# Moving the loads of a large key-value cache from SyncE's hardware queue to GpSimd's software queue in a two-block attention decode kernel

## The chip, the cores and the metric

The kernel runs on one core of one Trainium2 chip. The metric is the time of one execution in device microseconds (us). The profile's span is about 2 us shorter than the time (1326.8 us of span for 1329.2 us).

## The reference

One token attends to two caches, and the two outputs are concatenated. Block A is plain attention with 32 heads over 32,768 keys each. (Below, P·V is the product of a head's softmax weights with its values.) Block B has 32 query heads over 8 key heads and looks at the last 4,096 keys only.

```python
def _A_ref(x, k_cache, v_cache, wq, wo):          # x [1,1,512], caches [1,32,32768,128] bf16
    q = (x @ wq) ...                              # 32 heads of 128
    p = softmax(q · k_cache * Dh ** -0.5)
    return (p · v_cache) ... @ wo
# _B_ref: the same with 8 key heads, W = min(4096, max(256, Sk // 4)) last keys
return jnp.concatenate([a, b], axis=-1)
```

A's keys and values are 2 x 32 loads of 8.39 MB, 537 MB in all. Everything else (both wq, B's keys and values, both wo) is 33.6 MB.

## The kernel before

The program is a list of operations per engine; a wait is put in wherever an operation names another as its dependency. Each load names the operations that last read its buffer. `kbuf` has three thirds of 4.19 MB; a head of A takes two neighbouring ones, so every head shares one third with the next. `vbuf` holds one head's values, or B's values in two halves.

```python
    def load(self, dst, src, sem, *deps):
        self.op("sp", lambda e: e.dma_start(dst, src).then_inc(sem, 16), *deps)
    ...
    def k_thirds(self, g):
        return (1, 0) if g % 2 == 0 else (1, 2)

    def load_k(self, g, parts):                   # parts == 2 only for the last head
        ...
        if parts == 1:
            self.load(self.kbuf[:, w * lo:w * lo + 2 * w], src, self.mark("k", 0), *free)
            ...
        else:
            for i, t in enumerate(self.k_thirds(g)):
                self.load(self.kbuf[:, w * t:w * t + w], src[:, w * (t - lo):w * (t - lo) + w], self.mark("k", i), *free)

    def load_v(self, g):
        self.load(self.vbuf[:, :], self.kv_src("v", "A", g)[:, 0, :], self.mark("v", 0), *self.free["v"])
    ...
        for g in range(2):
            ...
            self.load_b("v", g)                   # block B's values
            self.emit_PV("B", g)
        ...
        for g in range(NQH):                      # block A, head by head
            self.load_k(g, 1 if g < NQH - 1 else 2)
            self.load_v(g)
            ...
            self.emit_unit("A", g)                # transposes of keys, scores
            self.emit_stats("A", g)
            self.emit_PT("A", g)
            self.emit_PV("A", g)
        for n in ("B", "A"):                      # output weights
            for part in range(len(self.WO_CUTS[n]) - 1):
                self.load_wo(n, part)
```

All loads but two of 1 KB are on one queue, SyncE's. So the order of this list is the order in which the loads are served, whatever each load waits for.

## Time and profile before

| | before |
|---|---|
| time, median | 1329.17 us (1329.11 to 1329.23) |
| bytes read, mean rate | 570.4 MB, 430 GB/s |
| busy: transfer engines, TensorE, VectorE | 99.6%, 73%, 57% |
| one head of A in the middle | 38.70 us (two loads of 19.35) |
| start of the first head of A, of the second-last, of the last | 83.45, 1246.03, 1279.71 us |

The numbers to read in such a profile are these: the share of the queue that carries the loads (the bound), the starts of heads (where time is lost or won), and the time from a load's issue to its landing (how far ahead it was asked for). The lines are in the prediction.

### The profile page before, as it was taken

The page shows a single profiled execution, that of the slowest core. Times are in us where ns is not written, and L with a number is a line of the kernel's source. Part 1 is how long each engine was busy: PE and PEld are TensorE (multiplying, and loading weights), DVE is VectorE, ACT ScalarE, POOL GpSimd, SP SyncE. Part 2 cuts the span into 40 slices and gives each one's busy share as a digit, 9 for nine tenths or more (in the row PEclk, how much of TensorE's full clock was granted, in tenths as well). Part 3 has the DMA queues.
Part 4 walks back from the last instruction along what each step waited for, and adds up shares of the span by engine and source line. Part 5 has one row for each costly group of instructions (what it writes and reads, how often), then busy time and mean ns, then how long its engine had stood idle before and what let it go on. Part 6 is the DMA issues. An engine that isn't in the chain of part 4 may idle for free.

```text
span 1326.8 us, 28797 instructions
## 1 busy us (share of the span) xinstructions
PE 964.5 (73%) x13436; PEld 679.5 (51%) x13436; DVE 749.8 (57%) x1345; ACT 54.8 (4%) x167; POOL 2.3 (0%) x17
## 2 busy tenths in 40 slices
PE   3757678777667877766787777678777767877786
PEld 3544455554445555444565544456554445655453
DVE  3645466665456666545666645566654556665473
ACT  0000000000000000000000000000000000000000
POOL 0000000000000000000000000000000000000000
PEclk9877788887788888778888878888887888888798
DMA  9999999999999999999999999999999999999998
GB/s 394 431 431 438 432 433 433 437 429 433 433 435 437 433 435 431 433 433 435 437 433 435 431 433 433 431 441 433 431 435 433 431 433 441 433 431 435 433 431 344
DMA packets 13079, 570.66 MB, mean 430 GB/s; under 512 B 1540, under 2 KB 1544, under 8 KB 1928
## 3 DMA queue, kind: packets, MB, share of 16 engines
q1 hardware_dynamic: 12776, 570.43, 99.6%
q8 instruction: 12, 0.20, 0.1%
q10 hardware_dynamic: 288, 0.00, 0.0%
q14 instruction: 3, 0.02, 0.0%
HBM read 570.43 MB, written 0.00 MB: 430 GB/s over the span
## 4 chain that ended last, share of the span: by engine, by line
DMA 70%; PE 28%; DVE 1%; issue 0%; SPq 0%; ACT 0%
DMA kbuf<-in_A_k_cache_dram 65%; PE psT L491 23%; PE psS L513 4%; DMA kbuf<-in_B_k_cache_dram 3%; DMA kbuf<-in_A_wo_dram 3%; DVE kt L494 1%; PE psACC L593 0%; SPq L286 0%; DVE oc_A L609 0%; ACT psb L541 0%; DVE tr_in L530 0%; PE psPT L565 0%; ACT ptsb L568 0%; PE psPT L655 0%; PE psG L620 0%
## 5 line engine op out<-in xcount | busy, mean ns | idle before, releaser
L494 DVE COPY kt<-psT 128x1024 bf16<-128x1024 bf16 x1056 | 655.2, 684 | 245.0 <-PE psT L491 243.1
L491 PE MATMUL psT<-ident,kbuf 128*128 128x128 bf16 x8448 | 579.2, 234 | 176.2 <-DMA kbuf<-in_A_k_cache_dram 164.4
L491 PEld LDWEIGHTS psT<-ident,kbuf 128*128 128x128 bf16 x8448 | 539.7, 106 | 268.2 <-DMA kbuf<-in_A_k_cache_dram 172.5
L593 PE MATMUL psACC<-vbuf,ptsb 128*4 128x512 bf16 (+1 forms) x2112 | 183.2, 523 | 23.1 <-ACT ptsb L568 21.3
L513 PE MATMUL psS<-kt,qw 128*32 128x512 bf16 x2048 | 157.6, 385 | 15.5 <-DVE kt L494 15.5
L607 DVE TENSOR_SCALAR oc_A<-psACC,hot_A 128x128 f32<-128x128 f32 x32 | 11.2, 351 | 247.8 <-PE psG L620 247.8
L593 PEld LDWEIGHTS psACC<-vbuf,ptsb 128*4 128x4 bf16 (+1 forms) x2112 | 60.0, 110 | 136.9 <-issue 87.2
L541 ACT ACTIVATE psb<-psS,nb_A 128x512 bf16<-128x512 f32 x32 | 22.0, 687 | 1169.9 <-DVE nb_A L540 1169.9
L513 PEld LDWEIGHTS psS<-kt,qw 128*32 128x32 bf16 x2048 | 34.0, 95 | 58.0 <-DVE kt L494 31.4
L620 PE MATMUL psG<-oc_A,hw 128*32 128x128 f32 (+1 forms) x128 | 19.3, 227 | 52.3 <-DVE oc_A L609 52.3
L620 PEld LDWEIGHTS psG<-oc_A,hw 128*32 128x32 f32 x128 | 11.4, 109 | 62.4 <-DVE oc_A L609 55.0
L565 PE MATMUL psPT<-ident,psb 128*128 128x128 bf16 x136 | 17.9, 274 | 34.0 <-ACT psb L541 34.0
L609 DVE SCALAR_TENSOR_TENSOR oc_A<-psACC,hot_A,oc_A 128x128 f32<-128x128 f32 x96 | 33.7, 351 | 3.4
L530 DVE TENSOR_REDUCE tr_in<-psS 128x1 f32<-128x512 f32 x34 | 23.5, 692 | 17.1 <-PE psS L513 17.1
L565 PEld LDWEIGHTS psPT<-ident,psb 128*128 128x128 bf16 x136 | 10.0, 116 | 37.0 <-ACT psb L541 36.7
L534 PE MATMUL psACC<-rows,tr_in 128*1 128x64 f32 x64 | 8.7, 217 | 25.6 <-DVE tr_in L530 25.6
L568 ACT ACTIVATE ptsb<-psPT 128x512 bf16<-128x512 bf16 x34 | 20.3, 597 | 28.2 <-PE psPT L565 28.2
L534 PEld LDWEIGHTS psACC<-rows,tr_in 128*1 128x1 f32 x64 | 2.7, 81 | 35.1 <-DVE tr_in L530 35.1
L538 PE MATMUL psACC<-mr_A,nscale 1*128 1x1 f32 x64 | 12.1, 256 | 9.8 <-DVE mr_A L537 9.8
L538 PEld LDWEIGHTS psACC<-mr_A,nscale 1*128 1x128 f32 x64 | 9.4, 183 | 15.7 <-DVE mr_A L537 15.7
L540 DVE COPY nb_A<-psACC 128x1 f32<-128x1 f32 x32 | 5.1, 158 | 15.0 <-PE psACC L538 15.0
L537 DVE TENSOR_REDUCE mr_A<-psACC 1x1 f32<-1x64 f32 x32 | 6.8, 213 | 11.7 <-PE psACC L534 11.7
(71 smaller groups left out, 75.1 us busy)
## 6 DMA issues: line engine op xcount, KB each, us to landing
kbuf<-in_B_k_cache_dram SPq DMA_DIRECT2D x2, 4096.0 KB, 32.5
vbuf<-in_B_v_cache_dram SPq DMA_DIRECT2D x2, 4096.0 KB, 23.6
kbuf<-in_A_k_cache_dram SPq DMA_DIRECT2D x2, 4096.0 KB, 22.0
vbuf<-in_B_wq_dram SPq DMA_DIRECT2D x1, 4096.0 KB, 12.3
vbuf<-in_A_wq_dram SPq DMA_DIRECT2D x1, 4096.0 KB, 32.4
kbuf<-in_B_wo_dram SPq DMA_DIRECT2D x2, 2048.0 KB, 33.1
kbuf<-in_A_wo_dram SPq DMA_DIRECT2D x1, 1408.0 KB, 28.5
kbuf<-in_A_wo_dram SPq DMA_DIRECT2D x1, 1024.0 KB, 30.6
```

The costliest lines, as they stand in the source:

```text
L491: inst = e.transpose(T[:, 128 * k:128 * k + 128], src[:, DH * k:DH * k + DH], self.ident[:, :])
L494: self.copies.append(self.op("dve", lambda v: v.tensor_copy(KT[:, :], T[:, :]), o, to="pe"))
L513: inst = e.matmul(self.S[32 * c:32 * c + 32, :], lhsT=win, rhs=self.kt[(bb + c // 2) % NKT][:, 512 * (c % 2):512 * (c % 2) + 512], start=b ...
L530: o = dve(lambda v: v.reduce_max(tr["in"][:, 0:1], self.S[:, :], axis=AXX), self.sdone, self.k_pool, to="pe" if name == "A" else None)
L534: o = self.op("pe", lambda e: e.matmul(self.ACC[0:1, 0:64], lhsT=tr["in"][:, 0:1], rhs=self.rows64[:, :], start=True, stop=True, skip_grou ...
L538: o = self.op("pe", lambda e: e.matmul(self.ACC[:, 64:65], lhsT=self.nscale[:, :], rhs=t["mr"][0:1, :], start=True, stop=True, skip_group_ ...
L541: self.sread = self.op("act", lambda s: s.activation(out=self.psb[:, :], in_=self.S[:, :], func=ACTF.Exp, bias=t["nb"][:, k:k + 1], scale= ...
L565: inst = e.transpose(PT[:, 128 * jj:128 * jj + 128], self.psb[:, 128 * jj:128 * jj + 128], self.ident[:, :])
L568: self.ptread = self.op("act", lambda s: s.activation(out=self.ptsb[:, :], in_=PT[:, 0:512], func=ACTF.Copy), self.psread, to="pe")
L593: inst = e.matmul(acc[32 * c:32 * c + rows, 0:512], lhsT=lhsT, rhs=rhs, start=begin, stop=end, tile_position=(0, 32 * c), skip_group_check ...
L609: o = self.op("dve", lambda v, src=src, hot=hot: v.scalar_tensor_tensor(out=oc, in0=src, scalar=hot, in1=oc, op0=ALU.mult, op1=ALU.add), p ...
L620: return self.op("pe", lambda e: e.matmul(self.G[0:32, c0 + c:c0 + c2], lhsT=win, rhs=t["oc"][g % 2][:, c:c2], start=False, stop=True, ski ...
```

## The change

The intent is to hand the bulk loads to GpSimd, which is idle, and whose queue has its descriptors (the orders to the transfer engines) built in software; the profile lists it as `software_dynamic`. GpSimd waits for each load's semaphore and raises another (`kasem`, `vasem`) for TensorE: a relay. The core of the diff (cut):

```diff
     def load(self, dst, src, sem, *deps):
-        self.op("sp", lambda e: e.dma_start(dst, src).then_inc(sem, 16), *deps)
+        self.op(self.queue, lambda e: e.dma_start(dst, src).then_inc(sem, 16), *deps)
...
+    def swload(self, which, g, dst, deps):
+        sem = self.swsem[which]
+        src = self.kv_src(which, "A", g)[:, 0, :]
+        self.op("pool", lambda e: e.dma_start(dst, src).then_inc(sem, 16), *deps)
+
+    def swlanded(self, which, g):
+        sem = self.mark(which, 0)
+        self.op("pool", lambda e: e.sem_inc(sem, 16), (self.swsem[which], 16 * (g + 1)))
...
-        if parts == 1:
-            self.load(self.kbuf[:, w * lo:w * lo + 2 * w], src, self.mark("k", 0), *free)
...
+        self.swload("k", g, self.kbuf[:, w * lo:w * lo + 2 * w], [self.free["k"][t] for t in self.k_thirds(g)])
+        if g:
+            self.swlanded("v", g - 1)
     def load_v(self, g):
-        self.load(self.vbuf[:, :], self.kv_src("v", "A", g)[:, 0, :], self.mark("v", 0), *self.free["v"])
+        self.swload("v", g, self.vbuf[:, :], self.free["v"])
+        self.swlanded("k", g)
...
+        self.queue = "pool"
...
-            self.load_k(g, 1 if g < NQH - 1 else 2)
+            self.load_k(g)
...
         self.loop = {}
+        self.queue = "sp"
```

B's loads and the output weights stay on SyncE. The last head's keys, two loads before, are one load now.

More of the change, by code (lines that the diff above doesn't have):

```diff
@@ L276, in alloc @@
         s = nc.alloc_semaphore
+        self.kasem = [s(f"kasem{i}") for i in range(2)]
+        self.vasem = [s(f"vasem{i}") for i in range(2)]
+        self.swsem = {w: s(f"swsem_{w}") for w in "kv"}
         self.ksem = [s(f"ksem{i}") for i in range(2)]
@@ L310, in k_thirds, with load_k @@
         return (1, 0) if g % 2 == 0 else (1, 2)
-    def load_k(self, g, parts):
+    def swload(self, which, g, dst, deps):
[5 more added lines that the diff above has]
+        self.op("pool", lambda e: e.sem_inc(sem, 16), (self.swsem[which], 16 * (g + 1)))
+    def load_k(self, g):
         w = HALF * DH
-        src = self.kv_src("k", "A", g)[:, 0, :]
         lo = min(self.k_thirds(g))
-        free = [self.free["k"][t] for t in self.k_thirds(g)]
-        if parts == 1:
-            self.load(self.kbuf[:, w * lo:w * lo + 2 * w], src, self.mark("k", 0), *free)
-            sem = self.mark("k", 1)
-            self.op("sp", lambda e: e.sem_inc(sem, 16))
-        else:
-            for i, t in enumerate(self.k_thirds(g)):
-                self.load(self.kbuf[:, w * t:w * t + w], src[:, w * (t - lo):w * (t - lo) + w], self.mark("k", i), *free)
+        self.swload("k", g, self.kbuf[:, w * lo:w * lo + 2 * w], [self.free["k"][t] for t in self.k_thirds(g)])
+        if g:
+            self.swlanded("v", g - 1)
     def load_v(self, g):
-        self.load(self.vbuf[:, :], self.kv_src("v", "A", g)[:, 0, :], self.mark("v", 0), *self.free["v"])
+        self.swload("v", g, self.vbuf[:, :], self.free["v"])
+        self.swlanded("k", g)
     WQ_SLOT = {"B": 0, "A": 1}
@@ L377, in plan @@
         self.emit_spread("B")
+        self.queue = "pool"
+        self.lsem = {"k": self.kasem, "v": self.vasem}
+        self.fill = {w: [0, 0] for w in "kv"}
         for g in range(NQH):
             self.loop = {"pe": g // 2, "dve": g // 2}
-            self.load_k(g, 1 if g < NQH - 1 else 2)
+            self.load_k(g)
             self.load_v(g)
+            if g == NQH - 1:
+                self.swlanded("v", g)
             self.emit_qcopy(g)
@@ L388, in plan @@
         self.loop = {}
+        self.queue = "sp"
         for n in ("B", "A"):
@@ L474, in emit_unit @@
             for half in range(2):
-                self.emit_T(HALF * lo + 16 * st + 8 * half, self.landed("k", g if name == "B" else i), t)
+                self.emit_T(HALF * lo + 16 * st + 8 * half, self.landed("k", g) if name == "B" else (self.kasem[0], 16 * (g + 1)), t)
             if n % 2:
@@ L595, in mm @@
             return inst
-        pv = self.op("pe", mm, self.landed("v", 0 if name == "A" else g), self.ptread, self.accread, to="sp")
+        pv = self.op("pe", mm, (self.vasem[0], 16 * (g + 1)) if name == "A" else self.landed("v", g), self.ptread, self.accread,
+                     to="pool")
         for i in (0, 1) if name == "A" else (g,):
```

## The prediction

> **What bounds the kernel now.** I read the busy rows and the queue table first, then the chain of work that ended last, then the waits, and last the timeline of one middle head and of the tail.
>
> ```profile
> DMA  9999999999999999999999999999999999999998
> ...
> DMA packets 13079, 570.66 MB, mean 430 GB/s; under 512 B 1540, under 2 KB 1544, under 8 KB 1928
> ...
> q1 hardware_dynamic: 12776, 570.43, 99.6%
> ...
> DMA 70%; PE 28%; DVE 1%; issue 0%; SPq 0%; ACT 0%
> ```
>
> The reader sees 16 transfer engines busy in every slice, one queue (SyncE's, q1) accounting for 99.6% of their time. The chain names PE for 28%, but only because a load is followed back to the read that freed its buffer. The waits settle it:
>
> ```profile
> PE psT L491 <- DMA kbuf<-in_A_k_cache_dram: 164.4, 31, 12.9
> ```
>
> TensorE stands still before the keys of nearly every head, about 5.3 us each; the loads are late, not the engines. The middle of the trace (one head, 39 us):
>
> ```profile
> core 0: us, PE busy (x) PEld busy (x) DVE busy (x) ACT busy (x) POOL busy (x), PEclk, DMA share, GB/s
> ...
> 600.00:639.00 39.00, 28.55 (x416) 20.65 (x413) 23.11 (x42) 1.59 (x5) 0.00 (x0) 0.87 1.00 434
> ```
>
> TensorE is busy 28.6 of 39 us, the transfer engines all of it, at 434 GB/s. Heads repeat every 38.7 us (TensorE starts at 626.71 here and at 665.42 for the next): two loads of 8.39 MB each, so 19.35 us a load. GpSimd is idle.
>
> How far ahead are the loads queued? The time from issue to landing less the 19.35 us of transfer is the time a load waited behind the one before it, which is the slack before the engines would run dry:
>
> ```profile
> vbuf<-in_A_v_cache_dram SPq DMA_DIRECT2D x32, 26.5
> ...
> kbuf<-in_A_k_cache_dram SPq DMA_DIRECT2D x31, 27.8
> ...
> x_B<-in_B_x_dram ACTq DMA_DIRECT2D x1, 1.0 KB, 12.5
> ```
>
> Slack is 26.5 - 19.35 = 7.2 us for values, 27.8 - 19.35 = 8.5 us for keys. The timeline agrees:
>
> ```profile
> 619.20 0.33 SPq L286 DMA_DIRECT2D vbuf<-in_A_v_cache_dram  x1
> ...
> 626.71 5.53 PE L491 MATMUL psT<-ident,kbuf 128*128 128x128 bf16 x64 [5.49 <-DMA kbuf<-in_A_k_cache_dram]
> ...
> 637.49 0.33 SPq L286 DMA_DIRECT2D kbuf<-in_A_k_cache_dram  x1
> ```
>
> The values' load is issued at 619.20, 7.5 us before the keys ahead of it land (626.71); the next keys' at 637.49, 8.6 us before those values land (626.7 + 19.35 = 646.1).
>
> **What the Trainium skill says.** (1) "DMA: Bandwidth & Descriptors", Issuing engines are not separate DMA queues: loads from any issuer run on the same 16 engines; another issuer saves only issue time. Consistent with this trace, where issuing costs 0.33 us every 19 us and q1 alone fills the engines. (2) Same page, Latency and other measured facts: first byte about 0.6 us for the hardware path, 1 us for the software path. No trace here has a software load. (3) Same page, Queues, rings and completion order: each engine takes turns between the queues with work, packet by packet. The trace agrees: x_B is 1 KB, yet took 12.5 us beside SyncE's loads. It is 8 packets per engine; a 32 KB row of SyncE's takes an estimated 1.21 us (32,768 B at 434/16 GB/s), and 8 x 1.21 plus some 2 us of start is about 12. (4) "SBUF — State Buffer", Who interferes with whom: a VectorE copy that uses both SBUF ports locks GpSimd out, and a software load then waits for its descriptors. That should not bite here: VectorE's large copies read PSUM, kt<-psT (684 ns each), and the page's two-port modes need SBUF on both sides.
>
> **The change part by part.**
>
> Removed: all 65 of SyncE's loads of the large cache (33 of keys, the last head's being cut in halves, and 32 of values); 64 take their place on GpSimd. Off the path: SyncE was idle otherwise.
>
> Added in the middle: GpSimd builds the descriptors of 64 loads. A row is 65,536 bytes per partition, so if a row stays one descriptor it is 128 of them plus completions. If that costs 1 to 3 us (my estimate, from the 1 us first byte of the skill), it lies inside the 7.2 us of slack; even adding a relay of 0.2 to 0.3 us (the load's semaphore is seen by GpSimd, which then raises one for TensorE), 3.3 < 7.2. Cost on the path: 0. The bytes and the rate should stay: 64 x 8.39 MB at 434 GB/s is 1238 us both ways. I allow 2 us for a slightly lower rate.
>
> Moved at the tail, and here I expect the cost:
>
> ```profile
> 1257.72 0.81 SPq L286 DMA_DIRECT2D kbuf<-in_A_k_cache_dram  x2
> 1277.76 0.33 SPq L286 DMA_DIRECT2D vbuf<-in_A_v_cache_dram  x1
> 1278.13 0.91 SPq L286 DMA_DIRECT2D kbuf<-in_B_wo_dram  x2
> 1288.79 2.23 SPq L286 DMA_DIRECT2D kbuf<-in_A_wo_dram  x5
> ```
>
> Before, SyncE's order kept the output weights (B then A, 4.19 MB each) behind the last values. After, SyncE holds no cache loads, so B's weights are asked for as soon as the second-last head's keys have been read out of their third, about 1267.5 (TensorE's transposes end near 1267.0). They then share the engines with the last keys, whose transfer starts at 1246.0 + 19.35 = 1265.4. And the last keys are now one load: TensorE can't start on a first half, as it did at 1279.7.
>
> By turns of packets, 64 KB against 16 KB rows, the keys keep 4/5, 347 GB/s. Until 1267.5 they move 0.9 MB alone; 7.48 MB at 347 take 21.6 us, to 1289.1. TensorE starts at 1289.4 instead of 1279.7. From that start to the last P·V took 24.5 us (1279.7 to 1304.25): 1313.9. The last values land at 1289.1 + 8.39 MB/347 = 1313.3, just in time. From P·V to the end was 22.55 us (1304.25 to 1326.8), of which 1.9 us were waits on A's weights (0.35 + 0.83 + 0.39 + 0.34); all bytes are in by about 1323.4, so these go: 1313.9 + 20.6 = 1334.5, **7.7 us more**.
>
> Sum: 1329.2 + 7.7 + 2 = 1339 us.
>
> **Rivals.**
>
> *Hidden anyway:* if a software load drains as one long turn, the weights wait; keys land at 1265.4 + 19.35 = 1284.8, and the end is 1284.8 + 0.3 + 24.5 + 20.6 = 1330.2, 3.4 us more: 1333 us.
>
> *Even shares:* if the software queue cuts rows to 16 KB, the weights take half for 19.3 us; keys land at 1294.4, and A's weights (asked for 9.1 us later) share with the last values, which land only at 1323.4. End 1323.6 + 20.6 = 1344.2, 17.4 us more: about 1347 us.
>
> *Software rate:* the skill gives 425 GB/s for its largest software load. Against 434 that is 2.1% of 1238 us, 26 us: about 1363 with the tail. For: nothing in this trace shows a software ring. Against: rows are 64 KB, so a descriptor comes only every 2.4 us per engine (65,536 B at 27.1 GB/s), which leaves ample time to fetch it.
>
> *GpSimd becomes the bound:* only if building one load takes over 7.2 us, about 50 ns for each of 144 descriptors. At 10 us each head would lose about (10 - 7.2) + (10 - 8.5) = 4.3 us, 138 us in all: about 1475. I give it 7%.
>
> *Faster:* the engines are already 99.6% taken; at most a few us are there. 1%.
>
> **Range and chances.** The middle cases run from 1333 to 1347; the lower rate at full size gives 1363. I choose 1330 to 1360. Over 2% slower is above 1355.8 us: the full rate loss (12%), GpSimd as the bound (7%), something unseen (3%): 0.22. Faster 0.01, the rest within 2%.
>
> **What would show it.** After: a software queue carries 64 loads (537 MB) with about 8,200 packets; the middle stays at 433 to 434 GB/s and heads at 38.7 us; keys' issue to landing stays above 21 us; GpSimd has next to no wait on it in TensorE's list. In the tail B's weights are issued near 1267 and the last head starts 5 to 15 us later than 1279.7. I am wrong if heads take over 39 us (rate or GpSimd), if the keys' issue to landing shrinks to 19 to 20 us (slack used up), or if the tail's order did not move.

## The result, and the profile after

The changed kernel takes 1340.3 us (1340.18 to 1340.42, 2 runs) against 1329.17: 1.0083 times as long, 95% interval 1.0054 to 1.0113. Such ratios are mean over mean, so not quite the ratio of the medians.

The page of the changed kernel: GB/s in 40 slices of 33.5 us, then the queues with packets, MB and share of the engines' time.

```profile
GB/s 394 430 338 434 434 439 435 423 437 431 437 439 433 425 437 433 435 435 437 425 437 433 435 437 435 425 437 433 435 435 435 427 437 433 435 435 437 425 432 289
...
q0 software_dynamic: 9216, 536.88, 92.7%
q1 hardware_dynamic: 3416, 33.56, 6.0%
```

The software queue carries A's 536.88 MB, and the slices of the middle move as many bytes as before. Only the third slice (338) and the last one (289; before 344) stand out. The issue-to-landing times stay above 21 us:

```profile
kbuf<-in_A_k_cache_dram POOLq DMA_DIRECT2D x32, 27.2
vbuf<-in_A_v_cache_dram POOLq DMA_DIRECT2D x32, 25.9
```

From the waits (engine, what it waited for, total us, times, longest us), two lines of the changed kernel:

```profile
PE psT L505 <- POOLq L322: 155.7, 31, 7.9
...
PE psACC L607 <- DMA vbuf<-in_B_v_cache_dram: 19.5, 1, 19.5
```

The first is the old wait on the keys under a new name: TensorE now waits for GpSimd's relay (L322), 155.7 us where it was 164.4. (The relay itself adds little: TensorE starts a middle head 0.60 us after the keys' last completion record, 632.87 to 633.47, and 0.50 us before the change, 626.21 to 626.71.) The second is new. Before, the wait for B's values was 1.0 us.

**The head of the program.** The timelines, first of the kernel before (SyncE's issues, then TensorE):

```profile
54.63 0.34 SPq L286 DMA_DIRECT2D kbuf<-in_A_k_cache_dram  x1
67.61 0.34 SPq L286 DMA_DIRECT2D vbuf<-in_A_v_cache_dram  x1
...
64.11 3.45 PE L593 MATMUL psACC<-vbuf,ptsb 128*16 128x512 bf16 x32 [1.02 <-DMA vbuf<-in_B_v_cache_dram]
```

and of the changed kernel (GpSimd's issues, then TensorE):

```profile
55.87 0.69 POOL L318 DMA_DIRECT2D kbuf<-in_A_k_cache_dram  x1 [52.94 <-PE psS L527]
87.06 0.53 POOL L318 DMA_DIRECT2D vbuf<-in_A_v_cache_dram  x1 [30.49 <-PE psACC L607]
...
83.54 3.19 PE L607 MATMUL psACC<-vbuf,ptsb 128*16 128x512 bf16 x32 [19.49 <-DMA vbuf<-in_B_v_cache_dram]
```

A's first keys are issued at the same point, about 55 us, while B's values are still coming in. Before, they queued behind them. Now they sit on another queue. B's values, needed first, land 19.4 us later; B's last P·V runs at 83.54 instead of 64.11; and A's first values, which need that buffer, are asked for at 87.06 instead of 67.61, when the keys are in and the engines have nothing left. The transfer view of 59.9 to 82.7 us, from the first key packet to the last, says how the engines were shared (packets, MB, share of the engines' time):

```profile
q0 software_dynamic: 139, 8.13, 82.7%
q1 hardware_dynamic: 135, 1.01, 10.6%
```

Nearly as many packets of one queue as of the other, and 8 to 1 in bytes: a row of keys, one packet, is 64 KB, a row of B's values 8 KB.

**The tail.** The starts of the second-last and the last head, before and in the changed kernel, and the changed kernel's issues of the weights on SyncE:

```profile
1246.03 6.43 PE L491 MATMUL psT<-ident,kbuf 128*128 128x128 bf16 x64 [4.83 <-DMA kbuf<-in_A_k_cache_dram]
...
1279.71 3.82 PE L491 MATMUL psT<-ident,kbuf 128*128 128x128 bf16 x64
```

```profile
1252.69 5.76 PE L505 MATMUL psT<-ident,kbuf 128*128 128x128 bf16 x64 [5.14 <-POOLq L322]
...
1295.06 5.09 PE L505 MATMUL psT<-ident,kbuf 128*128 128x128 bf16 x64 [7.87 <-POOLq L322]
```

```profile
1273.67 0.82 SPq L289 DMA_DIRECT2D kbuf<-in_B_wo_dram  x2
1305.62 2.23 SPq L289 DMA_DIRECT2D kbuf<-in_A_wo_dram  x5
```

B's weights are asked for 21.0 us after the second-last head's start; before, it was 32.1 us (1278.13 - 1246.03). From their first packet (1277.3 us) to 1294 us they shared the engines with the last keys (rows of 16 KB against 64 KB):

```profile
q0 software_dynamic: 95, 5.37, 74.4%
q1 hardware_dynamic: 100, 1.64, 23.0%
```

Again nearly packet for packet, and 5.37 MB against 1.64, 3.3 to 1. The last head starts 42.4 us after the one before it; in the kernel before it was 33.7.

**The sum.** The second-last head starts at 1252.69 instead of 1246.03, **6.7 us** lost at the head (6.8 already at the third head, 169.05 against 162.27, so the 28 heads between cost -0.1 us). From there to the end it is 85.8 us (1338.5 - 1252.69) instead of 80.8: **5.0 us** at the tail. Together 11.7 us of span between the two profiled runs. The 5.0 us are a net figure: B's projection, the product with B's weights near the end, took 3.40 us before at a granted TensorE clock of 0.55 (the share of full speed that the throttle allowed in that stretch), and 1.90 us in the changed kernel at 1.00. With equal clocks there the tail would have cost an estimated 6.5 us (5.0 + 1.5).

### The profile page after: what moved, and what is told of

Read it like the earlier page. It is cut to its first block, busy times and chain, and to the rows that moved or that the text cites. A ratio compares the mean times of both kernels' runs of the same rounds, so it can differ in the third digit from the quotient of the medians.

```text
span 1338.5 us, 28778 instructions
## 1 busy us (share of the span) xinstructions
PE 967.6 (72%) x13436; PEld 682.6 (51%) x13436; DVE 750.3 (56%) x1345; ACT 54.8 (4%) x167; POOL 36.3 (3%) x81
## 3 DMA queue, kind: packets, MB, share of 16 engines
q0 software_dynamic: 9216, 536.88, 92.7%
## 4 chain that ended last, share of the span: by engine, by line
DMA 63%; PE 27%; DVE 2%; issue 1%; ACT 0%; POOLq 0%
DMA kbuf<-in_A_k_cache_dram 63%; PE psT L505 23%; PE psS L527 3%; DVE kt L508 1%; PE psACC L607 0%; PE psPT L670 0%; PE psS L683 0%; DVE oc_A L624 0%; ACT psb L555 0%; POOLq L322 0%; DVE tr_in L544 0%; DVE pb L686 0%; PE psPT L579 0%; ACT ptsb L582 0%; PE psACC L670 0%
## 5 line engine op out<-in xcount | busy, mean ns | idle before, releaser
L505 PE MATMUL psT<-ident,kbuf 128*128 128x128 bf16 x8448 | 581.8, 235 | 168.6 <-POOLq L322 155.7
L607 PEld LDWEIGHTS psACC<-vbuf,ptsb 128*4 128x4 bf16 (+1 forms) x2112 | 59.9, 111 | 157.4 <-issue 90.5
L624 DVE SCALAR_TENSOR_TENSOR oc_A<-psACC,hot_A,oc_A 128x128 f32<-128x128 f32 x96 | 33.7, 351 | 3.4
L318 POOL DMA_DIRECT2D vbuf<-in_A_v_cache_dram x32 | 16.9, 530 | 656.3 <-PE psACC L607 656.3
L318 POOL DMA_DIRECT2D kbuf<-in_A_k_cache_dram x32 | 17.1, 535 | 592.7 <-PE psS L527 592.7
```

What stands on the lines that cost most here:

```text
L318: self.op("pool", lambda e: e.dma_start(dst, src).then_inc(sem, 16), *deps)
L505: inst = e.transpose(T[:, 128 * k:128 * k + 128], src[:, DH * k:DH * k + DH], self.ident[:, :])
L607: inst = e.matmul(acc[32 * c:32 * c + rows, 0:512], lhsT=lhsT, rhs=rhs, start=begin, stop=end, tile_position=(0, 32 * c), skip_group_check ...
L624: o = self.op("dve", lambda v, src=src, hot=hot: v.scalar_tensor_tensor(out=oc, in0=src, scalar=hot, in1=oc, op0=ALU.mult, op1=ALU.add), p ...
```

## The experiments

The theory after this reading (T1): the software queue by itself costs nothing; what costs is that loads in one order on one queue now stand on two, and overtake each other row by row. The rival (T2): software descriptors cost, in starts or in rate. All results were correct, and every kernel was timed against the kernel before on the same chip (median 1328.8 to 1329.2 in each batch). The changed kernel was not timed again with them, so differences from its 1340.3 us are between batches. The time is followed by the ratio's 95% interval.

### one_queue_sw: no second queue, all software

Every load except the two of 1 KB goes through GpSimd, in the old order; the last keys are in halves again.

```diff
-        self.queue = "sp"                 # plan()
+        self.queue = "pool"
-        self.constants()                  # moved behind the first four loads
...
+        if g == NQH - 1:                  # last keys: two loads, a semaphore each
+            for which, t in zip("kh", self.k_thirds(g)): ... dma_start of one third ...
...
-        self.queue = "sp"                 # before the output weights
```

> Every load but the two 1 KB ones goes through GpSimd's software queue, in the order of the kernel before; the last keys in two halves. No second queue is left that could overtake. Theory (only the order across two queues costs, the software queue is as fast): 1329.2 us plus about 0.5 to 1.5 us for later first issues: 1330 to 1331 us, heads 38.7 us apart. Rival (the software queue has a cost of its own at head or tail): 1335 us or more.

Measured: **1329.93 us** (0.9994 to 1.0019 of the kernel before). Its page:

```profile
q0 software_dynamic: 12704, 570.43, 99.5%
```

All 570 MB through software descriptors, relays included, cost 0.8 us by the medians, and 2.5 us at the interval's upper end, of the change's 11 us. T2 falls as the cause.

### hw_two_queues and hw_tail: the split without software

Starting from the kernel before, B's values and the weights go to ScalarE's hardware queue, the bulk stays on SyncE's, and the last keys are one load.

```diff
+        self.queue = "act"                # behind emit_qproj("A")
+        self.load_b("v", 0); self.load_b("v", 1)
+        self.queue = "sp"
...
-            self.load_b("v", g)          # in the loop over B's halves
...
-            self.load_k(g, 1 if g < NQH - 1 else 2)
+            self.load_k(g, 1)
             self.emit_unit("A", g)
+            if g >= NQH - 2:              # weights of B with head 30, of A with head 31
+                self.queue, n = "act", "BA"[g - NQH + 2]
+                for part in range(len(self.WO_CUTS[n]) - 1): self.load_wo(n, part)
+                self.queue = "sp"
```

> The kernel before, with no software queue at all: the large cache stays on SyncE's hardware queue, B's values and the output weights go to ScalarE's hardware queue, the last keys are one load. The same split into two queues as in the change. Theory (the split costs, not who builds the descriptors): about 1340 us, the idle stretch near 80 us and the slower last keys as in the changed kernel. Rival (software descriptors cost): 1329 to 1331 us.

Measured: **1337.81 us** (1.0053 to 1.008). The tail's cost is that of the change: 1334.9 - 1249.01 = 85.9 us from the second-last head's start. The head costs 3.0 us instead of 6.7, in another place than I expected. Here B's values, not A's keys, do the overtaking: they turn up on the second queue at 31 us beside B's second keys, which are read from 53.2 instead of 44.2 us, so A's first keys are issued at 64.5. (Long rows overtaking B's values on two hardware queues, the head's case in the change, has no run.) To have the tail alone, hw_tail leaves the head untouched:

> The kernel before with hardware queues alone: only the output weights move, to ScalarE's queue, asked for when their buffer is read out, and the last keys are one load. Head untouched. Theory: the tail's cost of the change, 5.0 us in its trace, and nothing else: 1329.2 + 5 = 1334.2 us. Rival (the tail's cost is the software queue's): 1329 to 1330 us.

Measured: **1334.47 us** (1.0032 to 1.006), 5.4 us over the kernel before, without one software descriptor. The sharing from the weights' first packet to 1288 us, bulk on q1 and weights on q10:

```profile
q1 hardware_dynamic: 103, 5.70, 75.7%
q10 hardware_dynamic: 108, 1.77, 23.9%
```

3.2 to 1, much as between software and hardware (3.3). For the tail it does not matter who builds the descriptors. What costs is the two queues with their row sizes and, since hw_tail has that too, the last keys' single load; tail_in_order and all_in_order below separate these.

### k0_small: the same queues, smaller rows

The changed kernel with head 0's keys cut into eight loads of 8 KB a row, the size of B's values (cut: the relay's count for the keys is raised by 7 x 16 to match).

```diff
+        if g == 0:
+            for i in range(8):
+                self.op("pool", lambda e, i=i: e.dma_start(
+                    dst[:, 4096 * i:4096 * i + 4096], src[:, 4096 * i:4096 * i + 4096]).then_inc(self.swsem["k"], 16), *free)
```

> The changed kernel, but the keys of head 0 are cut into eight loads of 8 KB a row, the packet size of B's values. Theory (engines take packets of the two queues in turns, so shares follow packet sizes): B's values now keep half of the engines instead of one ninth, land near 69 instead of 83.5 us, the first load of A's values is issued near 73 instead of 87 us, before the keys are all in, and the engines do not run empty: 1340.3 - 6.7 = 1333.6 us. Rival (the later queue simply goes first, whatever its packets): 1340 us, B's values landing at 83 us again.

Measured: **1335.09 us** (1.0037 to 1.0064), 5.2 us better than the change. From 60 to 64 us, while both queues have packets on most engines:

```profile
q0 software_dynamic: 104, 0.85, 51.6%
q1 hardware_dynamic: 103, 0.81, 48.4%
```

```profile
67.89 3.59 PE L615 MATMUL psACC<-vbuf,ptsb 128*16 128x512 bf16 x32 [3.73 <-DMA vbuf<-in_B_v_cache_dram]
```

Equal rows, equal shares. TensorE gets B's values at 67.89 us instead of 83.54, A's first values are issued at 71.79, and the second-last head starts at 1246.69, 0.7 us after the kernel before. So 6.0 of the head's 6.7 us go with the row size, the order of issue being unchanged. The cut into eight loads does not slow the keys by itself: their first packet comes at 59.85 us in both runs, and the eight issues, 4.33 us in all, are done long before 8.39 MB can be moved. With equal packet counts for rows of 8, 16 and 64 KB, the turns are one row each.

### head_in_order and head_wait: repairs of the head, one of them a miss

head_in_order puts A's first keys back on SyncE, behind B's values.

```diff
+        if g == 0:
+            self.queue = "sp"
+            self.load(self.kbuf[...], self.kv_src("k", "A", 0)[:, 0, :], self.mark("k", 0), *free)
+            self.queue = "pool"
+        else:
+            self.swload("k", g, ..., free)
```

> The changed kernel, but the keys of head 0 are loaded by SyncE's queue, behind block B's values; the other 63 loads of the large cache stay on GpSimd. Theory (two queues overtake each other): those keys no longer take 8 of 9 bytes from B's values, the first load of A's values is issued near 67 us instead of 87.1 us, the idle stretch of the transfer engines at 80 to 90 us goes, every head starts some 6.7 us earlier: 1340.3 - 6.7 = 1333.6 us. Rival (the software queue itself has a start-up cost or a lower rate): no change, 1340 us.

Measured: **1343.77 us** (1.0095 to 1.0126), worse than the change. B's values did come in time and A's first values were issued at 68.3 us, as expected. But these are now on the other queue than the keys ahead of them, and take turns with them, row by row of equal size:

```profile
95.61 5.32 PE L512 MATMUL psT<-ident,kbuf 128*128 128x128 bf16 x64 [24.68 <-DMA kbuf<-in_A_k_cache_dram]
```

The first head starts at 95.6 us instead of 83.45, the next keys are asked for at 106.5, and the engines idle then (264 GB/s from 100 to 120 us). I had moved the border between the queues by one load, and the overtaking moved with it. head_wait leaves the keys on GpSimd and lets them wait until B's values have landed.

```diff
+        if g == 0:
+            free += [self.b_landed]       # (vsem[1], 32)
```

> The changed kernel, but GpSimd issues the keys of head 0 only after block B's values have landed (near 64 us), so nothing overtakes them, and A's first values follow on the same queue. The engines stand empty about 2 us at that point. Theory: the head's cost falls from 6.7 to about 2.2 us: 1340.3 - 4.5 = 1335.8 us, the tail as in the changed kernel. Rival (the head's cost comes from the software queue's first loads): 1340 us or more. The run that put only these keys on SyncE made things worse (1343.8 us) because A's first values, on the other queue, then overtook the keys; here they cannot.

Measured: **1339.61 us** (1.0064 to 1.0095), 0.7 us better where 4.5 were expected. The head does improve, from 6.7 to 3.6 us (second-last head at 1249.62): the keys are issued at 64.72 us, the first packet comes 1.4 us later, and 2.5 us stand empty. The rest was given back behind the second-last head (88.1 us to the end instead of 85.8). There B's projection took 3.33 us instead of 1.90, with no wait of its own. The granted clock of the stretch, the third number from the right, differs (changed kernel, then head_wait):

```profile
1329.34:1331.24 1.90, 1.89 (x35) 0.66 (x32) 0.19 (x1) 0.00 (x0) 0.00 (x0) 1.00 0.07 20
...
1327.02:1330.35 3.33, 3.33 (x35) 0.93 (x32) 0.19 (x1) 0.00 (x0) 0.00 (x0) 0.56 0.02 5
```

The same goes for the other traces: 3.40 us at 0.55 (before), 3.27 at 0.57 (tail_in_order), 2.07 at 1.00 (all_in_order). So 1.4 us of what was given back are TensorE's clock at that moment, and not a transfer; why the clock is low in one run and full in another there is not shown.

### tail_in_order and all_in_order: repairs of the tail

tail_in_order issues the weights on the software queue, behind the last values.

```diff
         self.loop = {}
-        self.queue = "sp"
         for n in ("B", "A"):
             for part in range(len(self.WO_CUTS[n]) - 1):
                 self.load_wo(n, part)
+        self.swlanded("v", NQH - 1)
+        self.queue = "sp"
```

> The changed kernel, but both output weights are loaded by GpSimd's software queue, behind the last values; the last keys stay one load, the head stays as it is. Theory: the last keys land some 3.6 us earlier (no weights between their packets), last head's start at 1291.7 instead of 1295.1 us, end 3.4 us earlier: 1336.9 us. Rival (the tail's cost is only the lost first half of the last keys): 1340 us.

Measured: **1338.56 us** (1.0055 to 1.0083), 1.7 us better than the change; half of what was expected. The last head starts 38.7 us after the second-last instead of 42.4, as foreseen, but B's projection again took 3.27 us instead of 1.90 (clock 0.57, not 1.00), which eats 1.4 of the 3.7. all_in_order has this, the halves of the last keys, and head_in_order's repair of the head:

> The changed kernel with three repairs: head 0's keys behind B's values on SyncE, the output weights behind the last values on the software queue, the last keys in two halves. 63 of 64 heads' loads and all weights go through the software queue. Theory (only the order costs): back to the kernel before, 1329 to 1331 us. Rival (the software queue costs something by itself): 1333 us or more, the rest being its cost.

Measured: **1338.04 us** (1.0053 to 1.008). Against the expectation this is a miss, for the reason that head_in_order gave: 7.7 us are lost at the head (second-last head at 1253.75). Its tail is what I wanted to know: 1335.1 - 1253.75 = 81.4 us, 0.6 us over the kernel before. Order and halves together are nearly the tail's whole cost. The last head starts 42.4 us after the second-last in the change, 38.7 with the weights in order, 34.4 with the halves as well, 33.7 in the kernel before: 3.7 us of that delay are overtaking, 4.3 us the lost first half. So T1 explains only part of the tail; the rest is the merged load.

### pool_busy_1, pool_busy_a, pool_busy_b: how much may an issue cost?

The prediction held GpSimd's work hidden because a load waits 7 to 8 us behind the one before it. These runs put one, two or six scratch writes, 1.80 us each, ahead of every load of the changed kernel.

```diff
+        for i in range(n):                # n = 1, 2, 6
+            self.op("pool", lambda e: e.memset(self.idle[:, :], 0.0).then_inc(self.isem, 1), *deps, (self.isem, self.icount))
+            self.icount += 1
-        self.op("pool", lambda e: e.dma_start(dst, src).then_inc(sem, 16), *deps)
+        self.op("pool", lambda e: e.dma_start(dst, src).then_inc(sem, 16), (self.isem, self.icount))
```

> The changed kernel, but GpSimd writes a scratch tile of 128x2048 twice ahead of each of its 64 loads, an estimated 4.1 us (the 32x512 memset of the constants took 0.51 us). Results are unchanged. Theory (issue time on GpSimd is hidden while it stays under the time that a load waits behind the one before it, 6.5 us for values and 7.8 us for keys in the changed kernel's trace): no change, 1340 to 1342 us. Rival (the path runs through GpSimd's issue): 32 heads x 8 us = 262 us more.

> The same with six writes, an estimated 12.3 us ahead of each load, over the slack. Theory: heads become longer. The prediction's formula, (12.8 - 6.5) + (12.8 - 7.8) = 11.3 us a head, gives some 350 us more: about 1690 us. Rival within the theory (one late load per head sets the period, since a late key load also delays the release that the next one waits for): only the keys' excess and 1 to 2 us of start for each, 5 to 7 us a head, 155 to 217 us more: 1495 to 1557 us. If time stays at 1340 us, the slack is not what it was read as.

Measured: two writes **1367.52 us** (1.0267 to 1.0301), six writes **1521.17 us** (1.1422 to 1.146). Two writes delay an issue by 3.97 us:

```profile
632.57 3.67 POOL L321 MEMSET idle<- 128x2048 bf16 x2 [16.61 <-PE psACC L612]
636.53 0.53 POOL L323 DMA_DIRECT2D vbuf<-in_A_v_cache_dram  x1 [0.30 <-POOL idle L321]
```

That is less than the 6.5 us read as slack, yet it cost 27 us. The landing times mislead: a load has landed when the *last* of its 16 engines is done. The completion records of the changed kernel show the engines 2.1 us apart (3.2 us in the kernel before). The values issued at 626.89 us meet the first free engine at 630.72, 3.8 us later, not 6.0; and between an issue on an empty queue and its first packet lie 1.2 us. That leaves 2.6 us for values and, by the same count, 3.4 for keys. The third run was to test this:

> The changed kernel with one scratch write of 1.80 us ahead of each of GpSimd's loads (2.1 us with its wait). The two-write run (3.97 us more) cost 27 us although the landing times had promised 6.5 us of slack. New reading: what counts is the first of the 16 engines to finish the load before (3.8 us after the issue of values, 4.65 us after the issue of keys, not the 6.0 us of the last), less 1.2 us from an issue to its first packet: 2.6 us for values, 3.4 us for keys. Theory: 2.1 us fits, 1340 to 1342 us. Rival (each microsecond of GpSimd's issue costs in proportion, 27 us for 3.97 us): 1340.3 + 14 = 1354 us.

Measured: **1345.84 us** (1.0062 to 1.0149; four runs from 1335.7 to 1347.6). The result lies between the two theories. The run at 1335.7 us, 4.6 us below the change, has no trace. In the profiled run 20 of 29 heads in the middle stay at 38.7 to 38.8 us and 9 take 39.2 to 40.2, so 2.1 us is at the edge of the true slack, not under it. P·V takes 4.7 to 6.3 us from head to head (granted clock 0.76 and 0.58 in two of them), and the values are issued at its end, which moves that edge. The trace agrees for most: eight of the nine long heads follow a head whose P·V ended 32.1 us or more after that head's start; three others follow such a head and do not slip.

Six writes cost 181 us, 5.7 us a head (44.4 instead of 38.7). That speaks for the one-late-load reading (1495 to 1557 us) and against the prediction's sum of both excesses, which had given some 350 us. The mean granted clock was 0.774 in these runs against 0.83; its part is not separated. VectorE's large copies took 683 to 685 ns in all three runs, as in the change, so the writes did not slow them.

## Why the prediction was right or wrong

**The number** was right: 1339 us forecast, 1340.3 measured, inside the range and the likeliest class. That it came so close is luck: one cost of 6.7 us was left out, and two others were put too high.

- *What bounds the kernel, and the rate:* right. The middle stays at 38.70 us a head. The 2 us allowed for "a slightly lower rate" came to -0.1 us, and one_queue_sw shows the same over all loads. The rivals of a lower software rate and of GpSimd as the bound did not come. Of the signs named, one failed as worded: TensorE's waits on GpSimd come to 155.7 us instead of next to none, because the relay now stands for the late keys.
- *"Added in the middle ... Cost on the path: 0":* the outcome is right. An issue occupies GpSimd for 0.53 us, every one of the 62 in the middle, less than the 1 to 3 us estimated; waits of GpSimd for its descriptors, set aside in the prediction, do not show. The slack of 7.2 us was too large: the pool_busy runs put its edge near 2 us. At the upper end of my own estimate, 3.3 us with the relay, the change would by those runs have cost time in the middle. So the step "3.3 < 7.2" was wrong as a margin, and a cheaper issue covered it.
- *"Moved at the tail, and here I expect the cost":* the mechanism is right, and hw_tail and all_in_order show it. Its sizes are less so. With the head's delay taken off, B's weights were issued at 1267.0 us (1273.67 - 6.66), close to the 1267.5 forecast, but their first packet came 3.6 us after the issue, which the sum left out; then they took more than forecast, 3.3 to 1 instead of 4 to 1. The two nearly cancel: the last head's start was forecast 9.7 us later and came 8.7 us later (1295.06 - 6.66 - 1279.71). From there to P·V it was 25.5 us instead of 24.5. The mis-sized term is the last one, P·V to the end, 20.6 us forecast and 18.0 measured: B's projection took 1.90 us instead of 3.40, at the full clock, P·V 0.4 us less, and A's projection, now without waits, 3.66 us instead of the 4.32 of its five pieces. So 5.0 us instead of 7.7, and 1.5 of the difference is the clock, which neither the forecast nor the change deals with.
- *What was left out:* the head. The prediction looked for loads that the split frees from their old order, found the weights, and did not look at the other border, where A's first keys were freed from their place behind B's values. That step, the list of what moves, is the one that failed. It was worth 6.7 us, more than the tail. In the total it was mostly hidden by the 2 us for a lower rate and the 2.7 us too many at the tail.

## What to carry to other kernels

A queue is also an order: when some loads go to another queue, list every place where two neighbours of the old order now stand on different queues, and ask which is needed first. There the two take turns row by row, so the load with the longer rows wins the engines by the ratio of the rows; cutting the less urgent load into shorter rows was worth 5.2 us here. Merging two loads into one also costs the start on the first half, 4.3 us of the last head's delay here. The slack of a load is counted to the first transfer engine that runs dry, not to the last one that lands. And before a microsecond or two at the end of a kernel is put down to transfers, read the granted clock of that stretch: here it made 1.5 us.

## What the Trainium skill lacked or had wrong

- "DMA: Bandwidth & Descriptors", Issuing engines are not separate DMA queues, and Queues, rings and completion order: they say that several issuers interleave, packet by packet, and only save issue time. They do not spell out the cost for a load that is needed first (hw_two_queues, hardware queues alone: 3.0 us at its head), nor how many bytes a turn has (the packet is given in descriptors). Here a turn is one row: 95 to 100 packets for rows of 64 and 16 KB, 104 to 103 for rows of 8 KB each.
- Same page, Latency and other measured facts: first byte about 1 us for software and 0.6 us for hardware. From issue to first packet on idle engines these runs show 1.2 to 1.4 us for software (pool_busy_b, head_wait) and 0.95 us for hardware (hw_two_queues); on engines busy with another queue, 4.0 us (changed kernel, 55.87 to 59.85) and 3.5 us (hw_two_queues, 31.41 to 34.91).
- Same page, Measured: its table lists 16 MB in 79.0 us as 425 GB/s, but that quotient is 212, and its other rows too list about twice theirs. Loads of 8.39 MB on the software queue took 19.35 us each here, 434 GB/s.
- No page says how far the 16 engines of one load finish apart: 2.1 us in the changed kernel, 3.2 us in the kernel before, and 0.5 us when each load starts on empty engines (pool_busy_b).
